# Input loads re-queued, zero products around the first key weights, one copy of the last sums, and a new order table in a kernel of attention beside a spectral filter

## The chip, the cores and the metric

One core of a Trainium2 chip runs the whole program. The metric is the device time of one execution in microseconds; a version's time is the median of its runs. Besides TensorE (PE, with its weight loads listed apart as PEld) the core has VectorE (DVE), ScalarE (ACT), GpSimd (POOL) and SyncE (SP), which here only issues transfers. The five run their own instruction streams and meet through semaphores.

## The reference

The input `x` is 2048 tokens of 448 numbers in bf16. A softmax attention of 16 heads of 28 numbers and a spectral filter (a two-dimensional real Fourier transform, a product with a complex table, the transform back) work on the same `x`; a gate of one number per token mixes them.

```python
def _A_ref(x, wqkv, wo):
    B, S, D = x.shape
    H = 16; Dh = D // H
    qkv = (lambda x, *d: x.transpose(*d))((x @ wqkv).reshape(B, S, 3, H, Dh), 2, 0, 3, 1, 4)
    q, k, v = qkv[0], qkv[1], qkv[2]
    scale = Dh ** -0.5
    scores = jnp.einsum("bhqd,bhkd->bhqk", q, k) * scale
    p = _softmax(scores, axis=-1)
    o = jnp.einsum("bhqk,bhkd->bhqd", p, v)
    return (lambda x, *d: x.transpose(*d))(o, 0, 2, 1, 3).reshape(B, S, D) @ wo
...
def _B_ref(x, w_r, w_i):
    X = (lambda x, axes=(-2,-1): jnp.fft.rfft2(x.astype(jnp.float32), axes=axes))(x, axes=(-2, -1))
    X = X * W
    y = (lambda x, s, axes=(-2,-1): jnp.fft.irfft2(x, s=s, axes=axes).astype(jnp.bfloat16))(X, (S, D), axes=(-2, -1))
    return y
...
g = _sigmoid((x * gate_w).sum(-1, keepdims=True))
return g * a + (1 - g) * b
```

## The kernel before

`build` makes the tiles, then `head` (loads and constants), `make_units` (the small jobs) and `stream` (the order), and at last emits all instructions in the order found.

**Attention.** The 16 heads are taken in four groups of four, one head to 32 partitions, and the 2048 queries in four pieces of 512: sixteen *chunks* (group, piece). In a chunk every head meets sixteen blocks of 128 keys; such a pair is one score product, 512 columns from 30 rows into one PSUM bank (`score`), and up to four heads run beside each other in the array. The last two of the 30 rows keep the exponents small: they hold half the sum of squares of a query and of a key, and ones, which come from a constant row of `Wp` (`Wc`). The squares of a projected chunk are made by ACT in one instruction (`e_pj_sq`, L690), or by DVE in two (`e_pj_sd`, a copy at L696 and a product at L698); the last `qdn` chunks of queries take DVE's way.

Exponentials are made in two ways. ACT takes one, two or three banks in one instruction (L1263, 512, 1024 or 1536 columns) and writes them into the buffer `PA`, or at the start into `oT`, which is not yet in use. DVE takes one bank (L1287): a sum and a maximum, written as int16, whose bits read as bf16 are a rough power of two; POOL then makes two shifted copies of up to three such tiles (L1095), and all three versions are multiplied with the values, so that their errors cancel. A score made by ACT thus costs one product with the values (`bank<-PA,V`), one made by DVE costs three (`bank<-PD,V`).

When a chunk's products with the values are summed up in its bank, `normalise` copies the bank into `oraw`, sums four rows per head by small products (`bank<-cA,oraw`), takes the reciprocals, spreads them by products and multiplies into `oT`. For the last chunk the copy is halved: DVE takes 256 columns (L957) and ACT the other 256 (L958). After it only the output products of the last four token blocks, their scaling (L939 on ACT, L941 on DVE) and their stores are left.

**First keys.** For group 0 a unit `kw0` makes a weight for each key: sixteen products of 128 x 4 (`e_kw_pe`, `bank<-cA,kT`), a copy and a minimum on DVE, a transpose (`e_kw_tr`, L764), another minimum, products that spread it, a difference, and an exponential on ACT (L782). The values of group 0 wait for it.

**Filter.** It runs as matmuls between the chunks: F1 (128-point transforms of the token axis), F2 (over the 448 numbers), F3 with the table `Wf` and F5 (16 groups of frequencies), F6 (back over the 448 numbers). `o_t` adds gate, filter and attention for one block of 128 tokens.

**The head.** `x` comes in as five transfers: `xa` and `xb` (an eighth each), `x1`, `x2`, `x3` (a quarter each, 448 KB). `load` puts a transfer on SP's queue or on ACT's. In before SP's hold, in order, xa, xb, most of the constant `cA`, x1, x2, the row `Wp<-cWc`, x3, the values' weights `Wv` and the gate's weights (112 x 4 single numbers into the same tile); ACT's hold the identity and the key and query weights of group 0. `Wp` is cleared by POOL first (L445), and the transfer of its row waits for that; every projection waits for the row. PE transposes `x` in eight units `X0` to `X7` of eight transposes each (`e_xt_pe`, L672), and their evictions are on DVE, for X3 on ACT (L681).

**What sets the order.** `stream` is a list scheduler. It keeps for each engine the time at which it is free, by costs written down for each kind of instruction (`dve(n)`, `act(n)`, `cols(n)`, or a number in the unit's list of phases), and places step by step what can start first: scores (`do_s`, with the DVE share decided by `n_dve`, `dve_lead`, `pool_lead`), products with the values (`do_v`), or a unit whose target time has come. A unit's target is a share of T plus an offset of its own in the table `OFF`. When PE would, by these sums, stand idle for `zgap` or longer, `zeros` puts in products of a tile of zeros `zz`. Since all further placing depends on these sums, any cost, target or parameter that changes moves rows through the whole program.

Of the kernel before, what the change touches and what calls it, by code (L numbers as in the profile page):

```python
# [298 lines left out]
class Kernel:  # L299

    PAR = dict(T=368, margin=0, dve_lead=1.5, pool_lead=10, early=36.109, dmargin=0.1, join=0.6, veff=0.7, vnext=0, vnb=3, nfa=6, nfd=3, flush=0.954, hold=8.124, n_dve=280, late=31.911, fill=0, cp=3, slack=7.426, zgap=0.25, vurg=21.583, nfa2=5, nfd2=0, trk=0.4, vrk=2.7, fitm=0.043, ukeep=3, dkeep=0, k3=2, w3=0, w2=0.097, amax=3, ulate=10.503, dsolo=0, k21=0, a21=0, qdn=15)


    OFF = dict(X0=-12.17, X1=-2.46, X2=-38.11, X3=-5.88, X4=-30.11, X5=-0.77, X6=-10.66, X7=7.39, q0_0=-54.32, k0_0=-7.52, k0_0b=-2.5, k0_1=5.79,
               k0_2=17.41, k0_3=1.38, kw0=15.1, v0_0=27.93, v0_1=47.01, v0_2=47.26, v0_3=-0.66, q0_2=-7.12, q0_3=-0.38, gate=-37.65, F1_0=-11.56,
               F1_1=3.65, F1_2=-19.56, F1_3=13.58, F1_4=9.89, F1_5=-17.19, F1_6=-10.25, F1_7=3.57, F1_8=-11.23, F1_9=-27.33, F1_10=-25.08,
               F1_11=5.74, F1_12=47.64, F1_13=6.15, F1_14=-8.95, F1_15=-14.21, k1_0=-7.35, k1_1=18.2, k1_2=0.35, k1_3=-6.62, kw1=-20.58, q1_0=-5.84,
               v1_0=17.39, v1_1=4.38, v1_2=8.42, v1_3=0.39, q1_1=-5.74, q1_2=-14.52, q1_3=-2.84, F2_0=-52.08, F3_0=-5.71, F5_0=15.63, F2_1=-46.81,
               F3_1=-13.21, F5_1=25.59, F2_2=30.71, F3_2=-21.44, F5_2=-3.65, F2_3=-16.61, F3_3=-17.17, F5_3=-8.4, F2_4=14.45, F3_4=5.25, F5_4=-40.21,
               F2_5=0.02, F3_5=-0.1, F5_5=2.32, F2_6=22.29, F3_6=-19.52, F5_6=-8.84, F2_7=13.19, F3_7=-17.24, F5_7=3.35, F2_8=4.67, F3_8=-0.53,  # L310
               F5_8=8.74, F2_9=-7.29, F3_9=-34.2, F5_9=1.02, F2_10=20.34, F3_10=1.14, F5_10=-15.99, F2_11=-46.84, F3_11=-0.51, F5_11=17.43,
               F2_12=19.49, F3_12=-21.31, F5_12=0.11, F2_13=13.31, F3_13=7.7, F5_13=0.02, F2_14=-35.93, F3_14=-19.94, F5_14=9.92, F2_15=12.07,
               F3_15=0.6, F5_15=1.81, k2_0=-42.18, k2_1=-63.23, k2_2=-32.24, k2_3=-17.71, kw2=-5.31, q2_0=1.01, v2_0=22.01, v2_1=7.94, v2_2=33.73,
               v2_3=24.99, q2_1=-2.86, k3_0=12.61, k3_1=18.99, k3_2=5.17, k3_3=5.69, kw3=-49.09, q3_0=2.46, v3_0=9.64, v3_1=2.42, v3_3=-5.17,
               q3_1=-3.28, q2_2=-14.13, q3_2=-8.33, q2_3=-0.63, q3_3=-5.03, rg0=-5.48, rg1=-8.3, rg2=1.27, rg3=-5.65, F6_0=57.33, F6_2=-3.47,
               F6_3=6.32, F6_4=16.11, F6_5=-0.36, F6_6=60.6, F6_7=71.49, F6_8=5.75, F6_9=8.79, F6_10=53.62, F6_11=1.67, F6_12=14.97, F6_13=48.71,
               F6_14=-0.61, F6_15=34.0, o_0=1.52, o_1=0.87, o_2=-25.42, o_4=-12.01, o_5=12.58, o_6=-17.64, o_8=-36.7, o_10=-14.02, o_11=4.89,
               o_12=29.14, o_13=-34.54, o_14=9.53, o_15=2.41)
# [97 lines left out]
    def head(self):  # L416
# [19 lines left out]
        load("x1", *xl(4, 8), 4.6)  # L436
# [316 lines left out]
    def e_kw_pe(self, b, g):  # L753
        for i in range(16):
            self.mm(b[:, 4 * i:4 * i + 4], self.kT[g % 2][:, 128 * i:128 * i + 128], self.cA[:, 512:516])
# [7 lines left out]
    def e_kw_tr(self, b, g):  # L763
        self.nc.tensor.transpose(out=b.bitcast(BF16)[0:4, 0:128], in_=self.m1[:], identity=self.ident)  # L764
# [873 lines left out]
```

## Time and profile before

| | |
|---|---|
| three runs | 374.32, 373.74, 371.51 us (median 373.74) |
| profiled execution | 371.29 us, span 369.5 us |
| granted TensorE clock, mean | 0.995 |
| busy: PE, PEld, DVE, ACT, POOL | 362.7, 139.9, 324.2, 352.4, 325.4 us |
| exponentials on ACT (L1263) | 390 instructions, 338.2 us |
| exponentials on DVE (L1287) | 278 instructions, 183.4 us |
| shifted copies on POOL (L1095) | 188 instructions, 272.9 us |
| HBM read, written | 11.96 MB, 3.68 MB |

How to read the profile: it is one execution, and its times count from the start of its span; the 1.8 us between the span and the execution's own time lie around the first and the last instruction. In rows of groups the numbers behind the bar are busy time, mean nanoseconds of one instruction, and the idle time of the engine just before such instructions, with what ended most of it. In rows in order of time the first number is the start, the second the duration; a bracket tells how long the engine had stood idle and what ended it. A row of the kind `x4` stands for four instructions that follow each other, or run beside each other on PE. Instructions on ACT and DVE overlap at their ends, so the distance between two starts is shorter than a duration. The row PEclk gives the clock that the throttle granted to TensorE, in tenths, for forty slices of the span.

### The profile page before, as it was taken

How to read it: one execution, taken by the hardware profiler on the slowest of the kernel's cores; microseconds unless marked ns; L12 is line 12 of the kernel's file. 1: busy time of each engine (PE TensorE's matmuls, PEld its weight loads, DVE VectorE, ACT ScalarE, POOL GpSimd, SP SyncE). 2: the span in 40 equal slices, each digit the busy share in tenths (PEclk: the TensorE clock that was granted, in tenths of full speed). 3: DMA queues.
4: the chain of work that ended last, by engine and by line, in shares of the span. 5: the costliest groups of instructions: out<-in, count | busy, mean ns of one | idle time of the engine just before them, and what ended most of it. 6: DMA issues, size and time to landing. Idle time of an engine off the chain costs nothing.

```text
span 369.5 us, 15436 instructions
## 1 busy us (share of the span) xinstructions
PE 362.7 (98%) x6734; PEld 139.9 (38%) x6734; DVE 324.2 (88%) x565; ACT 352.4 (95%) x412; POOL 325.4 (88%) x262
## 2 busy tenths in 40 slices
PE   7999999999999999999999999999999999999995
PEld 3544342334343334335333334533433333333342
DVE  3797799998989889999999897799999999899873
ACT  2898999999999999999999999999999999999993
POOL 5998989999989989999999999889878999889980
PEclk9998999999999999999999999999999999999999
DMA  7556230000001102300212011002000000001001
GB/s 245 104 125 101 72 85 8 4 2 4 4 3 44 28 4 70 86 21 28 71 29 59 2 28 44 15 7 58 27 3 28 16 13 16 14 4 37 21 22 51
DMA packets 18969, 14.78 MB, mean 40 GB/s; under 512 B 7923, under 2 KB 18517, under 8 KB 18902
## 3 DMA queue, kind: packets, MB, share of 16 engines
q1 hardware_dynamic: 17686, 13.46, 14.2%
q8 instruction: 52, 0.85, 1.0%
q10 hardware_dynamic: 1216, 0.35, 0.4%
q14 instruction: 15, 0.12, 0.1%
HBM read 11.96 MB, written 3.68 MB: 42 GB/s over the span
## 4 chain that ended last, share of the span: by engine, by line
PE 88%; DVE 5%; ACT 2%; POOL 2%; DMA 1%; issue 1%; DVEq 0%; ACTq 0%; POOLq 0%
PE bank L394 87%; DVE PD L1287 2%; DMA Wp<-cWc 1%; ACT PA L1263 1%; PE bank L672 1%; POOL PD L1095 1%; ACT oT L1263 1%; DVE xt L924 0%; POOL Wp L445 0%; DVE AB L922 0%; POOL TT L899 0%; POOL TT L900 0%; ACT sq L690 0%; DVE sq L698 0%; DVE oT L975 0%
## 5 line engine op out<-in xcount | busy, mean ns | idle before, releaser
L1263 ACT ACTIVATE PA<-bank 128x1024 bf16<-128x1024 f32 (+1 forms) x390 | 338.2, 1050 | 1.7 <-PE bank L394 1.3
L1095 POOL TENSOR_SCALAR PD<-PD 128x1536 int16<-128x1536 int16 (+2 forms) x188 | 272.9, 1452 | 26.0 <-DVE PD L1287 9.4
L1287 DVE TENSOR_SCALAR PD<-bank 128x512 int16<-128x512 f32 x278 | 183.4, 683 | 14.9 <-PE bank L394 12.8
L394 PE MATMUL bank<-qT,kT 30*128 30x512 bf16 x1024 | 144.1, 385 | 0.1
L394 PE MATMUL bank<-PD,V 128*32 128x512 bf16 x834 | 124.4, 384 | 0.0
L394 PE MATMUL bank<-PA,V 128*32 128x512 bf16 x730 | 118.6, 383 | 0.0
L394 PEld LDWEIGHTS <-kT 30*128 30x128 bf16 (+1 forms) x1040 | 37.8, 91 | 114.9 <-issue 110.1
L394 PEld LDWEIGHTS <-V 128*32 128x32 bf16 x1580 | 33.0, 94 | 43.4 <-issue 38.9
L394 PE MATMUL bank<-xT,Wp 112*32 112x512 bf16 (+3 forms) x528 | 40.4, 385 | 1.1 <-DMA Wp<-cWc 1.1
L394 PE MATMUL bank<-Wv,xT 112*32 112x112 bf16 (+1 forms) x1024 | 18.5, 216 | 0.0
L394 PE MATMUL bank<-Wo,oT 128*32 128x448 bf16 x256 | 17.8, 355 | 0.0
L892 DVE TENSOR_TENSOR TT<-bank,Wf 128x900 bf16<-128x900 f32 x16 | 17.3, 1089 | 0.4 <-PE bank L394 0.2
L394 PEld LDWEIGHTS <-xT 112*32 112x32 bf16 x1024 | 14.2, 97 | 6.6 <-issue 5.8
L394 PEld LDWEIGHTS <-Wp 112*32 112x32 bf16 (+1 forms) x528 | 10.5, 96 | 15.1 <-issue 11.6
L696 DVE CAST sq<-bank 128x512 bf16<-128x512 f32 x15 | 10.3, 685 | 3.1 <-PE bank L394 3.1
L731 POOL TENSOR_TENSOR oT<-kT 128x512 bf16<-128x512 bf16 x12 | 12.4, 1039 | 0.6
L842 DVE CAST U__76<-bank 113x512 bf16<-113x512 f32 x16 | 10.7, 682 | 1.5 <-PE bank L394 1.5
L909 DVE CAST Z<-bank 113x512 bf16<-113x512 f32 x16 | 10.9, 686 | 1.2 <-PE bank L394 1.2
L394 PE MATMUL bank<-cG,TT 128*32 128x256 bf16 (+1 forms) x256 | 11.6, 275 | 0.1
L975 DVE TENSOR_TENSOR oT<-bank,oraw 128x512 bf16<-128x512 f32 (+1 forms) x19 | 11.1, 599 | 0.5 <-PE bank L394 0.5
L941 DVE TENSOR_TENSOR fin<-bank,g 128x448 bf16<-128x448 f32 x14 | 8.6, 619 | 3.3 <-PE bank L394 3.2
L711 DVE CAST kT<-bank 128x512 bf16<-128x512 f32 x15 | 10.2, 683 | 1.2 <-PE bank L394 1.1
(91 smaller groups left out, 283.3 us busy)
## 6 DMA issues: line engine op xcount, KB each, us to landing
cM<-cM SPq DMA_DIRECT2D x16, 128.0 KB, 3.0
cG<-cG SPq DMA_DIRECT2D x16, 128.0 KB, 2.0
Wf<-Wd SPq DMA_DIRECT2D x32, 56.2 KB, 2.3
out_dram<-fin SPq DMA_DIRECT2D x15, 112.0 KB, 1.7
xt<-in_A_x_dram SPq DMA_DIRECT2D x3, 448.0 KB
Z<-in_A_wqkv_dram SPq DMA_DIRECT2D x2, 294.0 KB
Wd<-in_B_w_r_dram SPq DMA_DIRECT2D x4, 112.5 KB, 10.9
Wd<-in_B_w_i_dram SPq DMA_DIRECT2D x4, 112.5 KB, 8.4
```

What stands on the lines that cost most here:

```text
L394: self.nc.tensor.matmul(out, lhsT=lhsT, rhs=rhs, start=start, stop=stop, skip_group_check=True, **k)
L696: self.nc.vector.tensor_copy(out=t, in_=b)
L711: self.nc.vector.tensor_copy(out=self.kT[g % 2][:, 512 * c:512 * c + 512], in_=b)
L731: self.nc.gpsimd.tensor_tensor(out=self.oT[:, 3, 512 * c:512 * c + 512], in0=k, in1=k, op=ALU.mult)
L842: self.nc.vector.tensor_copy(out=o, in_=b[0:113, :].rearrange("p (c g e) -> p c g e", c=4, g=16))
L892: self.nc.vector.tensor_tensor(out=self.TT[bg % 2][:].rearrange("p w r f -> p w (r f)").rearrange("p w (r f) -> p w r f", r=2), in0=bc_at( ...
L909: self.nc.vector.tensor_copy(out=self.Z[:, :, :, :, 8 * bg:8 * bg + 8].rearrange("p c t s e -> p c (t s) e"), in_=b[0:113, :].rearrange("p ...
L941: self.nc.vector.tensor_tensor(out=self.fin[k][:], in0=b[:, 0:448], in1=bc(self.g[:, t], 448), op=ALU.mult)
L975: nc.vector.tensor_tensor(out=self.oT[:, g, 512 * c + c0:512 * c + c1], in0=b[:, c0:c1], in1=oraw[:, c0:c1], op=ALU.mult)
L1095: nc.gpsimd.tensor_scalar(out=t[:, j, 0:n, :], in0=t[:, 0, 0:n, :], scalar1=float(sh), scalar2=1.0, op0=ALU.add, op1=ALU.mult)
L1263: nc.scalar.activation(out=buf, in_=src, func=ACT.Exp, scale=LN2 / 128.0)
L1287: nc.vector.tensor_scalar(out=dst, in0=self.bank[b], scalar1=C2, scalar2=0.0, op0=ALU.add, op1=ALU.max)
```

## The change

Five things change.

- `head`: x1 goes to ACT's queue, behind the query weights. x2 and x3 depend on the clearing of `Wp`, as its row does, and come behind that row. `Wv` and the gate's weights depend on nothing, so the planner places them ahead of the row on SP's queue.
- `e_kw_pe` and `e_kw_tr`: for group 0 a product of zeros of 512 columns goes ahead of the sixteen small products, and one of 252 columns ahead of the transpose, both into the unit's own bank. The planner's costs for the two phases go up to match, and its cost for the transposes of X0 goes from 0.056 to 0.12 each.
- `normalise`: the last chunk's sums are copied by ACT alone, 512 columns in one instruction.
- `PAR`: among others up to 300 scores may go to DVE instead of 280 (its lead shortened from 1.5 to 1), ACT squares eight of the sixteen query chunks instead of one (qdn 15 to 8), and zeros are put in from gaps of 0.42 instead of 0.25.
- `OFF`: another table of offsets, so nearly every unit stands elsewhere.

```diff
@@ -298,24 +298,24 @@
 
 class Kernel:
 
-    PAR = dict(T=368, margin=0, dve_lead=1.5, pool_lead=10, early=36.109, dmargin=0.1, join=0.6, veff=0.7, vnext=0, vnb=3, nfa=6, nfd=3, flush=0.954, hold=8.124, n_dve=280, late=31.911, fill=0, cp=3, slack=7.426, zgap=0.25, vurg=21.583, nfa2=5, nfd2=0, trk=0.4, vrk=2.7, fitm=0.043, ukeep=3, dkeep=0, k3=2, w3=0, w2=0.097, amax=3, ulate=10.503, dsolo=0, k21=0, a21=0, qdn=15)
-    OFF = dict(X0=-12.17, X1=-2.46, X2=-38.11, X3=-5.88, X4=-30.11, X5=-0.77, X6=-10.66, X7=7.39, q0_0=-54.32, k0_0=-7.52, k0_0b=-2.5, k0_1=5.79,
...
+    PAR = dict(T=368, margin=0, dve_lead=1, pool_lead=8.967, early=64.158, dmargin=0, join=0.406, veff=0.55, vnext=-1, vnb=2, nfa=6.208, nfd=2.827, flush=0.2, hold=4.933, n_dve=300, late=4.386, fill=1, cp=4.677, slack=8, zgap=0.42, vurg=21.991, nfa2=3.059, nfd2=0, trk=0.4, vrk=3.519, fitm=0.02, ukeep=3, dkeep=0, k3=2, w3=0, w2=0.02, amax=3, ulate=6.359, dsolo=0, k21=0, a21=0, qdn=8)
+    OFF = dict(X1=-13.09, X2=-24.51, X3=-3.84, X4=-1.98, X6=-19.75, X7=7.93, q0_0=6.15, k0_0=-6.62, k0_0b=14.98, k0_1=15.34, k0_2=11.57, k0_3=2.64,
...
 
 
     NB = 8
@@ -433,11 +433,7 @@
         load("wk0", rawv[:, :, 448:560], wv[:, :, 448:560], 2.8, "ACT")
         load("cA", self.cA[:, 128:521], C["A"].ap()[:, 128:521], 3.4)
         load("wq0", rawv[:, :, 0:112], wv[:, :, 0:112], 2.9, "ACT")
-        load("x1", *xl(4, 8), 4.6)
-        load("x2", *xl(8, 12), 6.0)
-        load("x3", *xl(12, 16), 7.4)
-        load("wv", self.Wv[:, :, 1:449], wv[:, :, 896:1344], 9.0)
-        load("gw", self.Wv[:, :, 0:1], self.gate_w.rearrange("(c p o) -> p c o", p=112, o=1), 9.0)
+        load("x1", *xl(4, 8), 3.9, "ACT")
         dep["x0"] = dep["xb"]
         dep["zz"] = P.add("DVE", 0.4, lambda: nc.vector.memset(self.zz, 0.0), key=-10)
 
@@ -446,6 +442,10 @@
 
         dep["ones"] = P.add("DVE", 0.7, lambda: nc.vector.memset(self.xT[96:128, 3, :], 1.0), key=-9)
         load("wpc", self.Wp[112:113, 3, :, :, :], C["Wc"].ap(), 2.4, deps=[m], key=-99.5)
+        load("x2", *xl(8, 12), 4.6, deps=[m])
+        load("x3", *xl(12, 16), 5.6, deps=[m])
+        load("wv", self.Wv[:, :, 1:449], wv[:, :, 896:1344], 7.0)
+        load("gw", self.Wv[:, :, 0:1], self.gate_w.rearrange("(c p o) -> p c o", p=112, o=1), 7.5)
         dep["mxz"] = P.add("POOL", 0.1, lambda: nc.gpsimd.memset(self.mx[:], 0.0), key=4)
         dep["xrz"] = P.add("POOL", 0.3, lambda: nc.gpsimd.memset(self.xr[:, :, 0:1], 0.0), key=-9)
 
@@ -514,7 +514,7 @@
         self.unit = unit
         for k in range(8):
             unit(f"X{k}", -50 + 2 * k,
-                 [("PE", 8 * 0.056, self.e_xt_pe, (k,), "full"),
+                 [("PE", 8 * (0.056 if k else 0.12), self.e_xt_pe, (k,), "full"),
                   ("DVE" if k != 3 else "ACT", 0.6 if k != 3 else 0.91, self.e_xt_ev, (k,))],
                  [dep["xa" if k == 0 else f"x{k // 2}"], dep["cI"], dep["ones"]])
 
@@ -567,9 +567,9 @@
                 return
             ks = [U[f"k{g}_{c}"] for c in range(4)]
             d = ks + [U["k0_0b"]]
-            unit(f"kw{g}", t0, [("PE", 0.45, self.e_kw_pe, (g,), "full"), ("DVE", 0.17, self.e_kw_rs, (g,)),
+            unit(f"kw{g}", t0, [("PE", 0.45 if g else 0.67, self.e_kw_pe, (g,), "full"), ("DVE", 0.17, self.e_kw_rs, (g,)),
                                 ("DVE", 0.2, self.e_kw_m1, (g,)),
-                                ("PE", 0.1, self.e_kw_tr, (g,), "full"), ("DVE", 0.3, self.e_kw_mm, (g,)),
+                                ("PE", 0.1 if g else 0.21, self.e_kw_tr, (g,), "full"), ("DVE", 0.3, self.e_kw_mm, (g,)),
                                 ("PE", 0.12, self.e_kw_bc, (g,), "full"), ("DVE", 0.2, self.e_kw_kd, (g,)),
                                 ("ACT", 0.3, self.e_kw_w, (g,))], d + [dep[f"vz{g % 2}"], dep["cA"]], rank=-1)
             for q in range(4):
@@ -751,6 +751,8 @@
 
 
     def e_kw_pe(self, b, g):
+        if g == 0:
+            self.mm(b, self.zz[:, 0:128], self.zz)
         for i in range(16):
             self.mm(b[:, 4 * i:4 * i + 4], self.kT[g % 2][:, 128 * i:128 * i + 128], self.cA[:, 512:516])
 
@@ -761,6 +763,8 @@
         self.nc.vector.tensor_reduce(out=self.m1[:], in_=self.rs[:].rearrange("p i h -> p h i"), axis=AX.X, op=ALU.min)
 
     def e_kw_tr(self, b, g):
+        if g == 0:
+            self.mm(b[:, 260:512], self.zz[:, 0:128], self.zz[:, 0:252])
         self.nc.tensor.transpose(out=b.bitcast(BF16)[0:4, 0:128], in_=self.m1[:], identity=self.ident)
 
     def e_kw_mm(self, b, g):
@@ -954,8 +958,7 @@
         if not last_n:
             o1 = [P.add("DVE", dve(512), lambda: nc.vector.tensor_copy(out=oraw[:], in_=pv), deps=[last] + prev, key=-3, then=freed)]
         else:
-            o1 = [P.add("DVE", dve(256), lambda: nc.vector.tensor_copy(out=oraw[:, 0:256], in_=pv[:, 0:256]), deps=[last] + prev, key=-3),
-                  P.add("ACT", act(256), lambda: nc.scalar.copy(out=oraw[:, 256:512], in_=pv[:, 256:512]), deps=[last] + prev, key=-3)]
+            o1 = [P.add("ACT", act(512), lambda: nc.scalar.copy(out=oraw[:], in_=pv), deps=[last] + prev, key=-3)]
 
         def sums(b):
             for k in range(4):
```

Counted over the two orders, ACT's exponentials of 1024 columns go from 344 to 353, those of 512 from 52 to 32, those of 1536 from 2 to 1, and its squares of 512 from 4 to 11; DVE's exponentials go from 278 to 283 and its two steps of squares from 15 to 8 each; POOL's shifted copies of 1536 columns go from 182 to 186, of 1024 from 4 to 2, of 512 from 2 to 4; PE's products with the values go from 1580 to 1590, and its zero products of 32 x 512 from 20 to 4.

The order of SP's requests at the start of the program, as a difference (`-` before, `+` the change; `xt` is x, 128x1792 a quarter of it, `Wp<-cWc` the row of ones; two requests in a row of one shape are printed as one with x2):

```order
 L404 DMA xt<-in_A_x_dram 128x896 x2
 L404 DMA cA<-cA 128x393
-L404 DMA xt<-in_A_x_dram 128x1792 x2
-L404 DMA Wp<-cWc 1x1024
-L404 DMA xt<-in_A_x_dram 128x1792
 L404 DMA Wv<-in_A_wqkv_dram 112x4x448
 L404 DMA Wv<-in_gate_w_dram 112x4x1
+L404 DMA Wp<-cWc 1x1024
+L404 DMA xt<-in_A_x_dram 128x1792 x2
 L404 DMA cC_80<-cC 128x128
 L404 DMA cA<-cA 128x132
```

The row of `Wp` stood behind two quarters of x and now stands behind the values' and the gate's weights; two quarters follow it. ACT's queue, in the change, opens with the third of the quarters:

```order
L404 DMA cA<-cA 128x128
L404 DMA Z<-in_A_wqkv_dram 112x4x112 x2
L404 DMA xt<-in_A_x_dram 128x1792
L440 ACT_TABLE_LOAD
L440 ACTIVATE geb<-zz 128x1
```

There the request for x1 follows those for the identity (`cA`) and for the key and query weights (`Z`), and stands ahead of the loading of the exponential's table.

On PE at the unit `kw0`, in the change (`kT` are the keys, `m` the minimum over a key's blocks):

```order
L394 LDWEIGHTS zz
L394 MATMUL bank<-zz 128x512
L394 LDWEIGHTS kT_72
L394 MATMUL bank<-cA,kT_72 128x4
...
L394 MATMUL bank<-qT_69,kT_72 128x512
L394 LDWEIGHTS zz
L394 MATMUL bank<-zz 128x252
L768 LDWEIGHTS m_109
L768 MATMUL bank<-cA,m_109 4x128
```

In before the sixteen small products followed a score, and filter products stood between them and the transpose; the two zero products are new, and scores stand between.

On ACT at the end of the program, before (`oraw` is the copy of the last sums, `fin` an output block):

```order
L1263 ACTIVATE PA<-bank 128x512
L1263 ACTIVATE PA<-bank 128x1024
L958 CAST oraw_97<-bank 128x256
L939 ACTIVATE fin_101<-bank,g 128x448
L939 ACTIVATE fin_103<-bank,g 128x448
```

and in the change:

```order
L1266 ACTIVATE PA<-bank 128x1024
L1266 ACTIVATE PA<-bank 128x512
L961 CAST oraw_97<-bank 128x512
L943 ACTIVATE fin_100<-bank,g 128x448
L943 ACTIVATE fin_103<-bank,g 128x448
```

The copy is twice as wide, and DVE's row `L957 CAST oraw_97<-bank 128x256` is gone from its engine.

28 lines of the change are left out of this document (14 added, 14 removed).

## The prediction

> **What bounds the kernel now.** I read the page first, then the ACT rows by form over the long middle, then the head, the one dip of the clock, and the tail.
>
> ```profile
> span 369.5 us, 15436 instructions
> PE 362.7 (98%) x6734; PEld 139.9 (38%) x6734; DVE 324.2 (88%) x565; ACT 352.4 (95%) x412; POOL 325.4 (88%) x262
> PEclk9998999999999999999999999999999999999999
> PE 88%; DVE 5%; ACT 2%; POOL 2%; DMA 1%; issue 1%; DVEq 0%; ACTq 0%; POOLq 0%
> ```
>
> Two engines are full at once. The chain that ended last is 88% PE, but a matmul row overlaps its neighbours, so 98% is not a measure. ACT is the firmer one: how far it is from its own pace can be counted. The next rows are ACT in order of time; the second number is an instruction's duration, the difference of two starts is its pace.
>
> ```profile
> 19.52 1.07 ACT L1263 ACTIVATE oT<-bank 128x1024 bf16<-128x1024 f32 x1
> 20.43 0.66 ACT L690 ACTIVATE sq<-bank 128x512 bf16<-128x512 f32 x1
> 20.90 1.10 ACT L1263 ACTIVATE oT<-bank 128x1024 bf16<-128x1024 f32 x1
> 21.81 1.11 ACT L1263 ACTIVATE PA<-bank 128x1024 bf16<-128x1024 f32 x1
> ...
> 12.55 1.45 ACT L1263 ACTIVATE oT<-bank 128x1536 bf16<-128x1536 f32 x1 [0.68 <-PE bank L394]
> 13.90 0.38 ACT L720 ACTIVATE sq<-bank 128x256 bf16<-128x256 f32 x1
> ```
>
> A 1024-wide instruction takes 1.07 to 1.11 us but the next starts 0.91 later; a 512-wide one is followed after 0.47, the 1536-wide one after 1.35. Between 42 and 340 us ACT ran these:
>
> ```profile
> L1263 ACT ACTIVATE PA<-bank 128x1024 bf16<-128x1024 f32 x304 | 284.2, 1109 | 0.3
> L1263 ACT ACTIVATE PA<-bank 128x512 bf16<-128x512 f32 x39 | 24.8, 677 | 0.0
> ```
>
> 304 x 0.91 + 39 x 0.47 = 295 of 298 us. So the middle has some 3 us to give and no more; nearly all the rest of what can move lies in the first 42 us and in the tail.
>
> In the head one chain sets the start. POOL clears Wp, then SP sends the row of ones into it, and PE waits for that row:
>
> ```profile
> 0.73 1.80 POOL Wp L445
> 3.40 4.85 DMA Wp<-cWc
> 8.30 1.49 PE bank L394 x26
> ```
>
> Then the clock: four windows of 3.41 us, one with the granted clock at 0.50 (the numbers behind the stretch: its length, then busy us and count of PE, PEld, DVE, ACT, POOL, then clock, DMA share, GB/s).
>
> ```profile
> 5.82:9.23 3.41, 2.26 (x48) 1.28 (x44) 0.93 (x2) 0.38 (x1) 1.34 (x2) 1.00 1.00 385
> 22.88:26.29 3.41, 3.22 (x71) 1.76 (x63) 3.38 (x10) 3.41 (x6) 3.16 (x4) 1.00 0.60 123
> 26.29:29.71 3.42, 3.42 (x49) 1.22 (x52) 1.97 (x3) 2.52 (x4) 3.34 (x2) 0.50 0.58 106
> 29.71:33.12 3.41, 3.41 (x185) 2.42 (x173) 2.63 (x7) 3.19 (x5) 2.35 (x3) 1.00 0.61 110
> ```
>
> ACT is busy for 2.52 of the slow window's 3.42 us, against 3.41 in the one before. What stands in its queue shows the price:
>
> ```profile
> 26.70 1.90 PE L394 MATMUL bank<-xT,Wp 112*32 112x512 bf16 x16
> 17.98 1.05 PE L394 MATMUL bank<-xT,Wp 112*32 112x512 bf16 x16
> 26.95 1.34 ACT L1263 ACTIVATE PA<-bank 128x1024 bf16<-128x1024 f32 x1
> 29.18 1.51 ACT L1263 ACTIVATE PA<-bank 128x1024 bf16<-128x1024 f32 x2 [0.90 <-PE bank L394]
> 30.91 1.02 ACT L1263 ACTIVATE PA<-bank 128x1024 bf16<-128x1024 f32 x1 [0.21 <-PE bank L394]
> ```
>
> The same 16 products take 1.90 instead of 1.05. The exponential at 26.95 is followed after 2.23 instead of 0.91, the two (512 and 1024 wide) from 29.18 after 1.73 instead of 1.38: 1.32 + 0.35 = 1.7 us lost on the bounding engine.
>
> **The change, part by part.**
>
> *ACT's work.* Counted over both orders: 9 more 1024-wide exponentials, 20 fewer 512-wide, one 1536-wide fewer, 7 more 512-wide squares (those of seven query chunks, which DVE did before in two steps each). 9 x 0.91 - 20 x 0.47 - 1.35 + 7 x 0.47 = **+0.7 us**, all on the path. DVE loses 14 instructions of 0.69 and gains 5 of 0.68; POOL gains 4 x 1.47 and 2 x 0.62 and loses 2 x 1.04:
>
> ```profile
> L1095 POOL TENSOR_SCALAR PD<-PD 128x1536 int16<-128x1536 int16 x182 | 267.5, 1470 | 25.2 <-DVE PD L1287 9.1 <-PE bank L394 2.1 <-DVE kc L750 0.8
> L1287 DVE TENSOR_SCALAR PD<-bank 128x512 int16<-128x512 f32 x278 | 183.4, 683 | 14.9 <-PE bank L394 12.8 <-POOL PD L1095 0.3
> L698 DVE TENSOR_TENSOR sq<-bank,sq 128x512 bf16<-128x512 f32 x15 | 10.4, 691 | 0.5
> ```
>
> That is -6.3 us on DVE and +5.0 on POOL, both costed at nothing: POOL stood idle 25.2 us before these very operations. Without that cover the 5.0 would come onto the path (a rival below).
>
> *The head.* SP's requests in before:
>
> ```profile
> 2.12 0.91 SPq L404 DMA_DIRECT2D xt<-in_A_x_dram  x2
> 3.40 0.29 SPq L404 DMA_DIRECT2D Wp<-cWc  x1
> 5.12 1.15 SPq L404 DMA_DIRECT2D Wv<-in_gate_w_dram  x1
> ...
> cC<-cC SPq DMA_DIRECT2D x1, 32.0 KB, 1.8
> Wv<-in_A_wqkv_dram SPq DMA_DIRECT2D x1, 392.0 KB
> xt<-in_A_x_dram SPq DMA_DIRECT2D x3, 448.0 KB
> ```
>
> Wp's row follows two quarters of x, 896 KB, through SP's queue. In the change it follows Wv (392 KB) and the gate's weights, and one quarter (448 KB) goes through ACT's queue beside them. The gate's request waits for the semaphore that Wp's row waited for, so it starts about 3.40 and holds SP for 1.15: Wp's row is asked for at 4.55. Bounds: with nothing in its way it lands 1.8 later (cC's time), 6.35, and then the first weights and the transposes decide at about 7.2, so -1.1; if all 840 KB drain at the old pace (896 KB ahead of a row that lands 4.85 after its request) and the gate's 448 tiny pieces take turns with x's large ones, it lands up to 1 us later than now, +1.0. I take **-0.4**: fewer bytes ahead, a later request, and four zero products (0.2 us) gone that stood behind the wait. The last two quarters of x are asked for about 4.9 and 5.3 instead of 2.6 and 3.7; their transposes start at 13 us now, so they are hidden until they are some 3 us late. The eight zero products between the first transposes filled a wait and cost nothing.
>
> [...] The row above, 4.85 us for 2 KB, bears out that what is ahead in the queues decides.
>
> *The zero products.* One full product of 512 columns ahead of the sixteen 4-column products on the first keys, one of 252 ahead of the transpose. At 0.22 us for 512 columns (the 16 products above: 1.05 for four rounds, the first 0.40) they cost 0.33 us of PE, in a stretch where ACT has work in hand. What can they buy?
>
> ```profile
> L394 PE MATMUL bank<-qT,kT 30*128 30x512 bf16 x10 | 2.1, 415 | 0.1
> L394 PE MATMUL bank<-cA,kT 128*128 128x4 bf16 x16 | 0.6, 165 | 0.0
> ```
>
> In the window before the slow one PE is listed busy 3.22 of 3.41 us, but with ten score products on 30 of 128 rows and sixteen products four columns long. Weighted by the part of the array in use, I estimate from the counts that window at 1.3 of 3.4 us, the window from 5.82, which was not followed by a slow one, at 2.0. The zeros add 0.33: 1.6, about midway. I take the slow window as gone, **-1.7**; bounds 0 (it falls all the same) and -2.6 (with the waits up to 42 us that follow it).
>
> [...]
>
> *The tail.* Before, two engines copy half of the last sums each, but one after the other:
>
> ```profile
> 362.27 0.37 ACT L958 CAST oraw<-bank 128x256 bf16<-128x256 f32 x1 [0.49 <-PE bank L394]
> 362.67 0.42 DVE L957 CAST oraw<-bank 128x256 bf16<-128x256 f32 x1 [1.86 <-ACT oraw L958]
> 363.15 0.26 PE L394 MATMUL bank<-cA,oraw 128*32 128x4 bf16 x16 [0.16 <-DVE oraw L957]
> ```
>
> DVE's half waits for ACT's. One ACT copy of 512 (0.60 to 0.66, as the squares) ends at 362.90 and PE starts at 362.95 instead of 363.15: **-0.2**.
>
> *The new order* moves thousands of rows. PE gets ten more products of weights (four abreast: 0.5 us) and stands in 357 groups of scores instead of 360: under 1 us either way. What it can change is how often ACT waits in the middle, at most -3 by the count above; a loss is not excluded and bounded at +5. I take **-0.5**, since seven chunks lose a DVE step ahead of their squares' product.
>
> Sum: +0.7 - 0.4 - 1.7 - 0.2 - 0.5 = **-2.1**, from the profiled execution's 371.29 (span and 1.8 around it) to 369.2. That execution lies 2.45 under the median of the three runs, 373.74; with 371.51 and 374.32 the four have a mean of 372.7, and a new median may fall on either group, so I forecast 372.7 - 2.1 = **370.6 us**.
>
> **Rivals.** *The clock falls all the same*: the zeros are too little, or the window lies otherwise. For: 1.6 is only midway. Against: the old stretch was the leanest. It gives the 1.7 back: 372.3.
>
> *The order fits better*: ACT's 3 us of waits in the middle vanish, DVE being 6.3 us lighter. Against: they lie scattered, 0.01 per exponential. 370.6 - 3.0 = 367.6.
>
> *POOL binds* (the slower side): between 42 and 340 us its five more busy us fall where exponentials made by DVE are already awaited, PD buffers come free later, PE's weight products stand behind them, and scores come late for ACT. The price is POOL's 5.0, with 0.4 for PE: 376.0. For: POOL is at 88%, its idle time lies in pieces. Against: it had 25.2 us. It decides once ACT's mean pace for 1024 columns rises by over 15 ns (5.4 over 357).
>
> *The clock rises a window later at the start*: without zeros between the first transposes the window that ends at 5.82 may not count as busy, and the next runs at half clock. In it PE is busy 2.26 us and waits 1.15 for Wp's row, so all but 0.5 is hidden: 371.1. [...]
>
> **How the numbers follow.** Forecast 0.42, clock falls 0.20, better order 0.20, POOL 0.13, late rise 0.05. One per cent, about what a measurement of this kernel can tell from no change, is 3.7 us: under 370.0 is faster, over 377.5 slower. The forecast's own range, 368.5 to 372.5, lies two fifths under 370.0: faster 0.17 + 0.20, rounded to 0.38; slower 0.08 of POOL's case with the unknown order; within 1% the rest, 0.54. The range for 8 in 10 goes from 366.6 (better order with the head's lower bound) to 375.2 (short of POOL's full price).
>
> **What would show it.** Right: no slice of the clock row under 9 after the start; PE's first product behind Wp's row before 8.3; ACT's 1024-wide pace in 42 to 340 not over 0.92; one oraw copy of 0.6 in the tail. Wrong: a 0.50 window again near 23 to 30 us; Wp's row landing after 8.7; waits of POOL's PD operations down to nothing while ACT waits for PE.

## The result and the profile after

The change made the kernel slower: 375.40 us median (373.01 to 377.24, 20 runs) against 372.18 us (369.58 to 375.09, 20 runs) for before on the same chip, a ratio of 1.0086 with a 95% interval of 1.0060 to 1.0112. The forecast was 370.6. (Runs over 1.5% above the fastest of their kernel are left out of all ratios here.) The profiled execution of the change took 376.86 us, 5.57 more than before's; its page opens so:

```profile
span 375.1 us, 15471 instructions
PE 363.5 (97%) x6730; PEld 142.7 (38%) x6730; DVE 318.8 (85%) x555; ACT 352.8 (94%) x407; POOL 331.0 (88%) x266
PEclk9699899999999999999999999999999999999999
PE 83%; DVE 9%; ACT 3%; DMA 2%; issue 2%; SPq 0%; DVEq 0%; ACTq 0%
```

The busy times are nearly those of before; the clock row has two dips, in the second and the fifth slice. ACT by form from 46 to 340 us, first before, then the change:

```profile
L1263 ACT ACTIVATE PA<-bank 128x1024 bf16<-128x1024 f32 x301 | 281.3, 1109 | 0.2
L1263 ACT ACTIVATE PA<-bank 128x512 bf16<-128x512 f32 x38 | 24.2, 678 | 0.0
```

```profile
L1266 ACT ACTIVATE PA<-bank 128x1024 bf16<-128x1024 f32 x306 | 286.6, 1142 | 0.1
L1266 ACT ACTIVATE PA<-bank 128x512 bf16<-128x512 f32 x22 | 15.2, 724 | 0.0
L690 ACT ACTIVATE sq<-bank 128x512 bf16<-128x512 f32 x6 | 4.4, 730 | 0.0
```

Idle time before ACT's exponentials is 0.2 and 0.1 us: past 46 us the new order is as tight as the old. The 5.6 us lie ahead of that. The head of the change, in order of time:

```profile
3.35 0.32 SPq L404 DMA_DIRECT2D Wv<-in_gate_w_dram  x1
3.78 0.31 SPq L404 DMA_DIRECT2D Wp<-cWc  x1
6.11 0.51 PE L394 MATMUL bank<-xT,Wp 112*32 112x256 bf16 x12 [0.18 <-DVE xT L679]
10.05 1.68 PE L394 MATMUL bank<-xT,Wp 113*32 113x256 bf16 x16 [3.43 <-DMA Wp<-cWc]
16.68 2.39 ACT L1266 ACTIVATE oT<-bank 128x1536 bf16<-128x1536 f32 x2 [1.38 <-PE bank L394]
```

PE waits 3.43 us for Wp's row and goes on at 10.05 instead of 8.30. The first exponential starts at 16.68 instead of 12.55: 4.13 of the 5.6 us are lost there, more than twice the row's own 1.75. The stretches of 3.41 us (length; busy us and count of PE, PEld, DVE, ACT, POOL; clock, DMA share, GB/s) tell the rest:

```profile
5.53:8.94 3.41, 0.91 (x19) 0.58 (x17) 1.13 (x2) 0.00 (x0) 0.17 (x1) 1.00 1.08 242
8.94:12.36 3.42, 2.31 (x25) 0.82 (x26) 0.29 (x1) 0.38 (x1) 3.29 (x3) 0.50 0.76 250
12.36:15.77 3.41, 3.41 (x34) 2.84 (x31) 1.52 (x3) 1.61 (x2) 3.41 (x7) 0.50 0.13 24
36.25:39.66 3.41, 2.06 (x63) 1.06 (x64) 1.81 (x5) 2.21 (x3) 3.13 (x4) 1.00 0.58 95
39.66:43.08 3.42, 3.42 (x30) 0.69 (x22) 1.58 (x4) 1.77 (x4) 0.67 (x1) 0.50 0.09 15
```

After the stretch of the wait (PE busy 0.91 of 3.41 us) the clock is 0.50 for two stretches, and the projections and transposes that lead to the first scores run slower: the sixteen products behind the row take 1.68 us and sixteen transposes 1.96, against 0.94 and 1.10 at full clock in e14. The second dip follows a stretch in which PE was busy 2.06 us. What it lacked stands in PE's rows there:

```profile
36.27 0.43 PE L394 MATMUL bank<-Wv,xT 112*32 112x113 bf16 x18
38.05 0.38 PE L394 MATMUL bank<-Wv,xT 112*32 112x113 bf16 x14 [1.35 <-issue]
```

In the middle of group 0's values PE stands still for 1.35 us, and "issue" means that it waited for nothing that the profile shows. Before has no such gap.

The clock also explains most of the spread of the runs (72% of the variance within a kernel). From a run's span and its mean granted clock follows how many stretches it spent at half clock: (1 - clock) x 2 x span / 3.41. A fraction of a stretch comes from the span's end, where PE is done: the last 0.93 us of the change's profile are at half clock. Over the 274 runs of before, the change and the fourteen kernels below that the ratios use, with a constant for each kernel, one such stretch costs 1.47 us (standard error 0.06). Before has 0.9 a run (107 runs; under half a stretch, called none below, in 48 of them), the change 2.55 (never fewer than one). The difference of 1.7 stretches is 2.5 us of the 3.3 us between the two means.

### The profile page after: what moved, and what is told of

Same layout as the page of the kernel before. It is cut to its first block, busy times and chain, and to the rows that moved or that the text cites. A ratio compares the mean times of both kernels' runs of the same rounds, so it can differ in the third digit from the quotient of the medians.

```text
span 375.1 us, 15471 instructions
## 1 busy us (share of the span) xinstructions
PE 363.5 (97%) x6730; PEld 142.7 (38%) x6730; DVE 318.8 (85%) x555; ACT 352.8 (94%) x407; POOL 331.0 (88%) x266
## 4 chain that ended last, share of the span: by engine, by line
PE 83%; DVE 9%; ACT 3%; DMA 2%; issue 2%; SPq 0%; DVEq 0%; ACTq 0%
PE bank L394 82%; DVE PD L1290 5%; DMA Wp<-cWc 2%; PE bank L672 1%; ACT oT L1266 1%; DVE AB L926 1%; ACT PA L1266 1%; DVE xt L927 1%; DMA cA<-cA 1%; DVE xt L928 1%; ACT sq L690 1%; DVE fin L945 0%; DVE oT L978 0%; DVE oraw L959 0%; DVE qT L709 0%
## 5 line engine op out<-in xcount | busy, mean ns | idle before, releaser
L1098 POOL TENSOR_SCALAR PD<-PD 128x1536 int16<-128x1536 int16 x192 | 278.2, 1449 | 26.0 <-DVE PD L1290 10.5
L1290 DVE TENSOR_SCALAR PD<-bank 128x512 int16<-128x512 f32 x283 | 186.0, 683 | 22.7 <-PE bank L394 18.8
L394 PE MATMUL bank<-qT,kT 30*128 30x512 bf16 x1024 | 141.2, 385 | 0.7 <-ACT PA L1266 0.4
L394 PE MATMUL bank<-PD,V 128*32 128x512 bf16 x849 | 126.0, 385 | 0.1
L394 PEld LDWEIGHTS <-Wp 112*32 112x32 bf16 (+1 forms) x528 | 10.1, 96 | 18.1 <-issue 12.2
L883 DVE CAST AB<-bank 128x448 bf16<-128x448 f32 x16 | 9.8, 616 | 1.2 <-PE bank L394 1.2
L394 PE MATMUL bank<-cG,TT 128*32 128x256 bf16 (+1 forms) x256 | 10.4, 274 | 0.2 <-ACT PA L1266 0.2
## 6 DMA issues: line engine op xcount, KB each, us to landing
Wd<-in_B_w_r_dram SPq DMA_DIRECT2D x4, 112.5 KB, 13.2
```

The costliest lines, as they stand in the source:

```text
L394: self.nc.tensor.matmul(out, lhsT=lhsT, rhs=rhs, start=start, stop=stop, skip_group_check=True, **k)
L883: self.nc.vector.tensor_copy(out=self.AB[bg % 2][:, 0:448], in_=b[:, 0:448])
L1098: nc.gpsimd.tensor_scalar(out=t[:, j, 0:n, :], in0=t[:, 0, 0:n, :], scalar1=float(sh), scalar2=1.0, op0=ALU.add, op1=ALU.mult)
L1290: nc.vector.tensor_scalar(out=dst, in0=self.bank[b], scalar1=C2, scalar2=0.0, op0=ALU.add, op1=ALU.max)
```

## The experiments

Theories at the start: the loads cost the time (L), or the new order does (O). To move a load without disturbing the planner, the order that it found is kept and only the head's load tasks are emitted in another sequence. To move instructions on PE, they are added or dropped when a task is emitted, with the planner's costs as they were. The lists of loads in the cuts below are the sequence in the change (`-`) and in the run (`+`). The kernels ran on three chips, each beside before, whose median there was 371.51 to 372.30 us; between experiments the ratios are safer than the medians.

**e1, the change with before's head loads.**

```diff
-        for t in self.P.order:
+        for t in arranged(self.P.order, self.dep):
...
+LOADS = ['xa', 'xb', 'wk0', 'cA', 'wq0', 'x1', 'x2', 'wpc', 'x3', 'wv', 'gw']
```

> The change with the order of its head loads put back to that of before (x1 and x2 ahead of Wp's row on SP's queue, then x3, the values' weights, the gate's weights; nothing on ACT's queue behind the query weights), every other row as in the change. In the change the first 1024-wide-or-more exponential starts at 16.68 us, 4.1 later than before's 12.55. Theory L (the loads cause it: Wp's row lets PE go on at 10.05 instead of 8.30 and a starved stretch drops the clock): PE goes on behind the row at 8.3 +- 0.3, the first exponential starts by 13.6, the time is 371.5 to 373.0, within 1 us of before. Theory O (the new order is worse by itself): the first exponential may start earlier, but the time stays at 374.5 or above, over 2 us above before.

375.99 us (6 runs), ratio to before 1.0123 (1.0069 to 1.0177). PE went on at 8.14 as theory L had it, yet the first exponential started at 14.15 and the time did not fall. Its profile has the same gap, longer, and three half-clock stretches (from 9.07, 36.38 and 39.79):

```profile
8.14 0.29 PE L394 MATMUL bank<-xT,Wp 113*32 113x256 bf16 x4 [1.52 <-DMA Wp<-cWc]
14.15 2.39 ACT L1266 ACTIVATE oT<-bank 128x1536 bf16<-128x1536 f32 x2 [0.77 <-PE bank L394]
36.30 0.53 PE L394 MATMUL bank<-Wv,xT 112*32 112x113 bf16 x14 [1.94 <-issue]
```

Theory L alone is wrong.

**e2, before with the change's head loads** (same edit with the other sequence, x1 on ACT's queue).

> The kernel before with the head loads of the change (values' and gate's weights ahead of Wp's row, x1 on ACT's queue, x2 and x3 behind the row), every other row as before. Theory L: PE goes on behind the row at 9.7 to 10.4, the first exponential starts at 14.3 or later, the time is 2 to 4 us above before, 374 to 376. Theory O: the time is within 0.8 us of before.

373.12 us (12 runs), 1.0025 (0.9994 to 1.0057): between the two. PE went on at 9.42, the first exponential came at 13.66, 1.1 us later than in before, and half-clock stretches were no more frequent (1.0 a run). In the old order the loads cost about their own lateness and nothing else. Its profile has a gap at the values too, a shorter one, which comes up again under e5:

```profile
31.52 0.23 PE L394 MATMUL bank<-Wv,xT 112*32 112x113 bf16 x4 [0.59 <-issue]
```

**e3, the change with the gate's weights asked for last.**

```diff
-   ... 'wv', 'x1', 'gw', 'wpc', 'x2', 'x3'
+   ... 'wv', 'x1', 'wpc', 'x2', 'x3', 'gw'
```

> The change with one request moved: the gate's weights (448 single numbers) behind x3 instead of ahead of Wp's row. Theory G (the 448 small pieces hold the row back): PE goes on behind the row at 8.8 or earlier, and the time falls by 1.5 to 3 us below the change. Theory B (the bytes ahead of and beside the row do it, 392 KB of the values' weights and 448 KB of x1): PE goes on at 9.4 or later and the time stays within 0.8 us of the change.

376.00 us (12 runs), 1.0083 (1.0046 to 1.0119). PE went on at 9.27, inside the 9.3 to 10.1 of the other kernels with the change's loads (e5 10.10, e6 9.44, e7 9.60). That is over G's 8.8 and under B's 9.4, so neither theory met its number for the row; the time stayed, as B had it. The 448 small pieces explain at most a small part of the delay.

**e4, the change with x1 on SP's queue behind the row.**

```diff
-   ... 'wv', 'x1', 'gw', 'wpc', 'x2', 'x3'
+   ... 'wv', 'gw', 'wpc', 'x1', 'x2', 'x3'
```

> The change with x1 taken from ACT's queue and put on SP's queue directly behind Wp's row; values' and gate's weights stay ahead of the row. Theory B: the row comes at least 1 us earlier, 9.0 or before, since 448 KB no longer run beside it; the transposes of x1 then start later than in the change. Theory G: the row comes at 9.4 or later.

371.94 us (12 runs), 1.0006 (0.9964 to 1.0049): 3.5 us under the change (3.0 by the ratios). In its profiled execution, one of its slowest at 375.97, PE went on at 8.10; in e9, which has the same loads, at 7.47. Both are earlier than theory B's 9.0. Six of the runs had no half-clock stretch, which no run of the change managed. So the 448 KB running beside the row, asked for by ACT, hold it back by 1.2 us or more.

**e5, the change with the eight zero products of the head back.**

```diff
         v = b.bitcast(BF16).rearrange("p (t c q) -> p t c q", t=2, c=4)
+        for _ in range(2 if k == 1 else 0):
+            self.mc(b, self.zz[:, 0:128], self.zz)
```

> The change with the eight zero products of 32 x 512 put back ahead of the second unit of transposes, where before had them. In the change's runs the granted clock averages 0.985 to 0.991 in 19 of 20, which is two to three stretches of 3.41 us at 0.50, against 0 to 2 in before; each costs about 1.5 us by the runs. Theory Z (without those zeros the stretch before Wp's row counts as idle and PE runs at half clock from 9 us on): one stretch fewer on average, mean clock 0.991 to 0.996, time 373.5 to 374.5. Rival (the 3.4 us wait for the row decides, zeros or not): clock and time as in the change, 375 to 376.

376.6 us (6 runs), 1.0106 (1.0064 to 1.0149), 2.6 stretches a run: theory Z falls, 0.6 us of zeros do not make up for a wait that was 3.62 us here. But it showed something else. The gap in the values moved by eight products, 18 done and 14 left before, 10 and 22 now; in e7, with two products fewer ahead, it moved two the other way, 20 and 12:

```profile
35.29 0.33 PE L394 MATMUL bank<-Wv,xT 112*32 112x113 bf16 x10
37.56 0.48 PE L394 MATMUL bank<-Wv,xT 112*32 112x113 bf16 x22 [1.94 <-issue]
```

```profile
34.83 0.43 PE L394 MATMUL bank<-Wv,xT 112*32 112x113 bf16 x20
36.48 0.34 PE L394 MATMUL bank<-Wv,xT 112*32 112x113 bf16 x12 [1.22 <-issue]
```

Each product comes with a weight load, so eight products are sixteen instructions, as many as were added. The gap sits at a fixed number of PE's instruction stream, not at a datum. Counted over the listed products and loads, it lies behind the 1218th (607 products, 611 loads) in all six profiles of the change's order with these narrow values. In e2 and e8, which have the old order, it lies behind the 962nd, 256 earlier, and lasts 0.59 and 0.25 us: the old order has it too, only shorter, though the next expectation says that no run with the old order has it.

**e6, the change with group 0's values in wide products.** 64 products of 128 weights' columns and 64 loads instead of 256 and 256, same sums.

```diff
-            self.mc(b[:, n * t:n * t + n], ...
+            (self.mc if g else self.mm)(b[:, n * t:n * t + n], ...
```

> The change with the values of group 0 made by 64 products of 128 columns instead of 256 of 32 (same sums, a quarter of the instructions). In the change PE stands still for 1.35 us in the middle of these products (36.70 to 38.05), waiting for nothing that the profile shows, and the clock is 0.50 from 39.7 to 43.1; the same gap is in all three variants with the new order and in no run with the old. Theory F (256 dense products with 256 weight loads outrun PE's own instruction stream): the gap is gone, no half-clock stretch follows it, and the time is 373 to 374. Rival (PE waits there for data or a bank): a gap of over 1 us remains at these products and the time stays at 375 to 376.

372.51 us (12 runs), 1.0024 (1.0001 to 1.0048): 2.9 us under the change (2.3 by the ratios), no gap at the values, and no half-clock stretch between 13.8 and 368 us of its profile. That is what theory F expected of the gap and the clock. The head's half-clock stretch is still there; 1.8 a run.

**e7, the change without its two zero products.**

> The change without its two zero products beside the first keys. Theory N (they do nothing for the clock here, since its dips come from the wait for the row and from the gap in the values): the same clock as the change and the time within 0.8 us of it, 374.6 to 376.2. Rival, my forecast's own step (they keep a stretch near 23 to 30 us from counting as idle): a half-clock stretch shows there, mean clock 0.981 to 0.987, and the time rises by 1.2 us or more, to 376.6 or above.

375.88 us (6 runs), 1.0103 (1.0061 to 1.0146), 2.6 stretches a run as in the change, and 1.00 in every stretch from 13.2 to 371.6 us of its profile. The zeros do nothing here.

**e8, before with the two zero products and one copy of the last sums.**

> The kernel before with the two zero products beside the first keys and the last sums copied by ACT alone, in before's order. Half of before's runs show one stretch at half clock or more (mean 0.9 a run), 1.5 us each. My forecast's step: the stretch at 26 us goes, the runs move to a mean clock of 0.998 or above and the time falls by 1.0 us or more; the tail is 0.2 us shorter from the last exponential to PE's sums (2.51 us in before). Rival: the clock's dips stay as frequent, and the time is within 0.6 us of before.

370.89 us (12 runs), 0.9981 (0.9946 to 1.0015). Eight of twelve runs had no half-clock stretch, against 48 of 107 for before: in the direction of my step, and too few to tell. The tail is told by its rows:

```profile
363.75 0.58 ACT L962 CAST oraw<-bank 128x512 bf16<-128x512 f32 x1 [0.49 <-PE bank L394]
364.38 0.26 PE L394 MATMUL bank<-cA,oraw 128*32 128x4 bf16 x16
```

From the copy's start to PE's sums 0.63 us, against 0.88 in before (362.27 to 363.15): 0.25 shorter.

**e9, the change with both repairs** (e4 and e6 together).

> The change with both repairs: x1 on SP's queue behind Wp's row (alone it brought the median from 375.4 to 371.9) and group 0's values in 64 wide products (alone 372.5). Theory (two separate causes, the row's wait and the gap in the values): the two add up in the clock, no half-clock stretch in most runs, mean of slow stretches 1 or fewer, time 369.8 to 371.0, below the kernel before. Rival (both act on the same loss): 371.5 to 372.5.

370.76 us (12 runs), 0.9966 (0.9938 to 0.9994), 0.7 stretches a run: the loss is gone, and the two repairs, 3.5 and 2.9 alone, give 4.6 together (by the ratios 3.0, 2.3 and 4.5).

```profile
7.47 0.94 PE L394 MATMUL bank<-xT,Wp 113*32 113x256 bf16 x16 [0.85 <-DMA Wp<-cWc]
11.81 2.39 ACT L1266 ACTIVATE oT<-bank 128x1536 bf16<-128x1536 f32 x2 [0.68 <-PE bank L394]
```

With the row at 7.47 and the clock at 1.00 the new order reaches its first exponential 0.74 us before the old one did.

**e10, before with the wide values.**

> The kernel before with group 0's values in 64 wide products, nothing else. Before shows no gap at these products. Theory F (the wide form helped the change because it closed the gap in PE's instruction stream): no gain here, within 0.7 us of before. Rival (it helped because it takes work from PE): the same 2 to 3 us gain as in the change, 369.5 or below.

374.65 us (12 runs), 1.0045 (1.0013 to 1.0076): slower, which neither theory had. 384 instructions fewer at 30 us shift all that follows in PE's stream, and now a gap opens beside a later group's values, 200 us on; ACT behind it takes 2.83 us for two exponentials that need 1.82:

```profile
236.22 0.38 PE L394 MATMUL bank<-PA,V 128*32 128x512 bf16 x1
237.24 0.39 PE L394 MATMUL bank<-PD,V 128*32 128x512 bf16 x1 [0.64 <-issue]
...
235.17 1.96 ACT L1263 ACTIVATE PA<-bank 128x1024 bf16<-128x1024 f32 x2
238.00 1.95 ACT L1263 ACTIVATE PA<-bank 128x1024 bf16<-128x1024 f32 x2 [0.87 <-PE bank L394]
```

The rival's gain of 2 to 3 us did not come. The gap, 1.0 us from start to start, is a part of the 1.7 us lost by the ratio; the rest stays open, and with it what less work for PE would be worth alone.

**e11, the change with the wide values and the row asked for first** (x1 on SP's queue here too).

```diff
-   nc.gpsimd.memset(self.Wp[:].bitcast(F32), 0.0)
+   [nc.gpsimd.memset(self.Wp[:, k].bitcast(F32), 0.0) for k in (slice(3, 4), slice(0, 3))]
-   ... 'wv', 'x1', 'gw', 'wpc', 'x2', 'x3'
+   ... 'wpc', 'x1', 'x2', 'x3', 'wv', 'gw'
```

> The change with the wide values, and Wp's row asked for before x1, x2, x3, the values' and the gate's weights: POOL clears the quarter of Wp that holds the row first (one quarter of 1.8 us), so SP can ask for it at about 2.1 us. Theory L2 (what is ahead of and beside the row delays it): PE goes on behind the row by 7.0 instead of 10.05, without a wait of over 1 us, the first exponential starts by 13.0, no half-clock stretch at 9 us, time 369.0 to 370.5. Rival (the next input decides, the query weights' copy on POOL or x's transposes): PE waits as long for that, the first exponential starts at 13.5 or later, 370.5 to 372.

370.41 us (12 runs), 0.9950 (0.9917 to 0.9983): the lowest median here, ahead of both kernels. PE no longer waits for the row at all (the sixteen products run together), only 0.40 us for the query weights' copy:

```profile
6.11 0.63 PE L394 MATMUL bank<-xT,Wp 112*32 112x256 bf16 x16
7.14 0.83 PE L394 MATMUL bank<-xT,Wp 112*32 112x512 bf16 x12 [0.40 <-POOL Wp L473]
11.06 2.39 ACT L1266 ACTIVATE oT<-bank 128x1536 bf16<-128x1536 f32 x2 [0.68 <-PE bank L394]
```

**e12, before with the early row, the wide values, the two zero products and one copy.**

> The kernel before with the same early row, the wide values, the two zero products beside the first keys and one copy of the last sums. If the change's order is worth 0.5 us, as I forecast, this is 0.3 to 1.0 us above e11; if the order is worth nothing the two are within 0.5 us; both lie below before by 1 us or more if the row's wait (1.15 us and more there) is paid in full.

371.15 us (12 runs), 0.9966 (0.9936 to 0.9996), no half-clock stretch in any run, and 0.74 us above e11. That fits the order's 0.5, but e10's gap is in it too (it carries the wide values; 0.30 us at 235.59), so the order's share is not settled by it.

**e13, the change with before's loads and the wide values.**

> The change with before's order of head loads and with group 0's values in 64 wide products. Alone the old loads brought the row as early as x1's move did (8.14 and 8.10 us) and yet no time (375.99 against 371.94 in the medians, six and twelve runs). Theory P (the old loads are as good for the head, and only the gap in the values kept e1 slow): with the gap closed the time is that of e9, 370.3 to 371.5. Rival (the old loads cost the new order something else, later inputs of the values or of x): 372.0 or above.

372.87 us (12 runs), 1.0023 (0.9992 to 1.0054): the rival's number, no gain over e6, though PE went on at 8.57. It still stood 1.79 us for the row, and from 9.91 the clock was 0.50 for a stretch. An earlier row was worth little here: the stretch around the wait stayed thin (PE busy 1.63 of 3.42 us).

**e14, the change with the wide values and the wait filled with zero products.**

```diff
+        for _ in range(24 if (half, k) == (0, 2) else 0):
+            self.mm(b[:, 256:512], self.zz[:, 0:128], self.zz[:, 0:256], start=False, stop=False)
```

> The change with the wide values, and 24 zero products of 128 x 256 (2.6 us of PE) between the first projection's twelve products and the four that wait for Wp's row, so that PE is busy while it waits; the row comes as late as in the change (9.3 to 10.1). e6 without them has 1.8 half-clock stretches a run and 372.5. Theory C (the wait costs more than its length, because the idle stretch is followed by half clock): the stretch from about 9 to 13 us runs at full clock, one half-clock stretch fewer a run, first exponential by 13.9 instead of 15.0, time 370.8 to 371.6. Rival (the lateness alone costs, the clock follows something else): clock and time as e6, 372.2 or above.

370.58 us (12 runs), 0.9973 (0.9936 to 1.0011), 0.6 stretches a run against e6's 1.8: theory C. The first pair of stretches is e6's, the second that of e14:

```profile
6.94:10.35 3.41, 0.91 (x26) 0.54 (x24) 0.00 (x0) 0.38 (x1) 3.33 (x4) 1.00 0.97 285
10.35:13.77 3.42, 3.42 (x36) 2.30 (x25) 1.35 (x3) 1.48 (x2) 2.65 (x5) 0.50 0.49 135
```

```profile
6.08:9.49 3.41, 3.41 (x45) 2.71 (x48) 0.69 (x1) 0.00 (x0) 2.37 (x2) 1.00 1.09 263
9.49:12.91 3.42, 3.42 (x63) 2.38 (x55) 1.97 (x4) 1.99 (x3) 3.34 (x4) 1.00 0.52 186
```

```profile
6.55 2.79 PE L394 MATMUL bank<-zz 128*128 128x256 bf16 x24
9.28 0.94 PE L394 MATMUL bank<-xT,Wp 113*32 113x256 bf16 x16
13.33 1.45 ACT L1268 ACTIVATE oT<-bank 128x1536 bf16<-128x1536 f32 x1 [0.68 <-PE bank L394]
```

The products behind the row run at 9.28, as late as ever (e6: 9.44), but at full clock, and the first exponential starts at 13.33 instead of e6's 14.99: 1.5 of those 1.66 us are the clock's.

## Why the prediction was wrong

*ACT's work, +0.7, and the tail, -0.2*, were right: the counts hold, the middle is as tight as before, and the copy to PE's sums takes 0.65 us in the change (0.63 in e8) against 0.88.

*The head, -0.4, bounded at +1.0*, failed first. It took the row's time from the bytes ahead of it on its own queue and let x1 run "through ACT's queue beside them" at no price. The row was asked for at 3.78, earlier than the 4.55 that I had worked out (the gate's request held SP for 0.32 us, not 1.15), and yet it took 6.23 us to land instead of 4.85:

```profile
3.78 6.23 DMA Wp<-cWc
```

PE went on 1.1 to 1.75 us later (e2; the change), and x1 was the main reason: 7.47 and 8.10 with it behind the row (e9, e4), 9.3 to 10.1 with it beside; the gate's place made little difference (e3). What x1 beside the row costs is shown by these runs; how the transfers of two queues mix is not.

*The clock* was the larger failure. I priced the wait as hidden ("all but 0.5 is hidden"; *the clock rises a window later*, 371.1, chance 0.05). That rival blamed the zero products missing from the head; putting them back changed nothing (e5). The wait's price is not its length: in the change the stretch in which PE waits is followed by half clock, and the first exponential came 4.13 us late for a row 1.75 us late. e14 takes the clock's part away and leaves the lateness. In the profiles here the granted clock changes at the ends of stretches of 3.41 us, whose place scatters from run to run (the first starts at 4.3 to 7.3 us), and PE was not idle in the stretches ahead of the half clock: in the change 0.50 followed 0.91 and even 2.06 busy us of 3.41. And the -1.7 for the dip at 26 us was read from one execution of before; 48 of 107 have no half-clock stretch, so the mean loss from all of before's is 0.9 x 1.47 = 1.3 us, and the most that zeros at any one place could have bought is less than that. In the change they bought nothing (e7). The estimate behind that term, 1.3 and 2.0 of 3.4 us weighted by the array in use, was not tested by any run.

*The new order, -0.5*, was bounded at -3 to +5 for ACT's waits in the middle. The middle was fine. What the order cost was at its start: it sets the units of group 0's values so close together that PE stood still among them, 1.35 us in the change and 1.94 in e1. I had no term for that, since no row of before shows it; e5 and e7 show that the gap sits at an instruction's number, e6 that fewer instructions for the same sums close it. The profile page's queue of 52 instruction transfers with 0.85 MB is 16.4 KB each. The gaps lie whole multiples of 256 listed products and loads apart (behind the 962nd, the 1218th, and in e10 and e12 the 8898th). A dense run of 32-column products with their loads takes 360 instructions in 3.42 us in the change's stretch from 32.83 on:

```profile
32.83:36.25 3.42, 3.42 (x186) 2.47 (x174) 2.64 (x7) 3.42 (x6) 3.30 (x2) 1.00 0.56 110
```

The traces hold each of these transfers (queue q8) with its time. In the change one runs from 35.58 to 36.50, and PE goes on at 38.05; in all ten profiles with such a gap PE goes on 1.27 to 1.65 us after a transfer has landed. The last 128 products ahead of the gap and their loads took PE 2.39 to 2.45 us in the change's order, and 3.06 in e2 and e8, where the gap is short. In before the same place was reached after 4.41 us, partly at half clock, 2.45 us after the landing, and there is no gap. I take it that PE waits there for its next instructions; which instructions a transfer holds, the trace does not say, so that is a reading and not shown.

*POOL binds* and the other rivals were not it. POOL stood idle 26.0 us before its shifted copies in before and in the change alike. Of the signs that I had named, the single copy and the absence of a 0.50 window between 23 and 30 us came out right, and PE's start behind the row (10.05, not before 8.3), its landing (10.01, after 8.7) and the clock row came out wrong.

In sum, on the means: 1.7 more half-clock stretches x 1.47 = 2.5 us, and 0.8 for the lateness and the gap themselves, less what the rest of the change gains. With both repaired (e9) the change stands 1.2 us below before at equal clock (369.8 against 370.9 by the fit). But 0.74 of that is its earlier first exponential, and it has the wide values besides, so no run separates what the change's other parts gain; the forecast had put ACT's work, the tail and the order at 0.0 together.

Open: why a stretch with 2.06 or 2.16 busy us was followed by half clock at the values, and one with 2.16 or 2.17 in the head was not, nor one with 2.20 at the values in e7; why before's stretch with 3.22 was; why e2, whose wait of 2.73 us is as long as e6's 2.50, has 1.0 half-clock stretches a run and e6 1.8; and how much of e4's gain needed luck in where the stretches fell.

## What to carry to other kernels

Price a wait of TensorE by what the clock does after it, not by its length: in the profiles here unfilled waits in the head of 0.85 and 1.15 us were not followed by half clock, and those of 1.38 to 3.62 us were, in all but one (e2, 2.73). Such a stretch cost about 1.5 us, and zero products in the wait bought that back (e14). A transfer that must land first is asked for first, and nothing large is put beside it on another engine's queue: PE waited 3.43 us for the row in the change, 1.49 (e4) and 0.85 (e9) with x1 behind it, and not at all with the row asked for first (e11). Before a scheduler may set many short matmuls back to back, look at how many instructions that is (360 in 3.42 us ahead of the change's gap); the same sums in a quarter of the instructions removed a gap of 1.35 us that no semaphore explained (e6), but moved the rest of the stream, which in the other order opened a gap elsewhere (e10).

## What the runs showed of the hardware

The stretches of the granted clock are 3.41 us long and start at another place in every profile (the first at 4.3 to 7.3 us of the span in the sixteen profiles). In the head, stretches at full clock with 0.54 (e7) to 1.87 us (e8) of listed PE time were followed by half clock, those with 1.94 (e2) to 3.42 (e14) were not. A gap in PE's instruction stream, 0.25 (e8) to 1.94 us (e1, e5) long, keeps its place by count, behind the 962nd, 1218th or 8898th listed product or load, whole multiples of 256 apart, and so moves one for one against the data as instructions are added or dropped ahead of it (e5, e7); in the old order the wide values opened one of 0.64 us, 200 us later (e10).
